# Attention units regrouped: four heads of two neighbouring rows in place of eight heads of one row

## The chip, the cores and the metric

The kernel runs on one core of a Trainium2 chip. The metric is the device time of one execution in microseconds. The core has a matrix engine (TensorE, PE in the profile; its weight loads are listed apart as PEld), a vector engine (VectorE, DVE), a scalar engine (ScalarE, ACT), GpSimd (POOL) and SyncE (SP), which issues most of the transfers. Each engine takes its instructions in program order; an instruction that is not ready holds up everything behind it on that engine.

## The reference

Three layers follow one another. The change touches only the first, attention over keys and values that are averaged in groups of eight:

```
B, H, S, D = q.shape                      # 8, 8, 576, 64
k_p = k.reshape(B, H, S // 8, 8, D).mean(axis=3)     # 72 pooled keys
v_p = v.reshape(B, H, S // 8, 8, D).mean(axis=3)
scores = (q @ k_p.transpose(0, 1, 3, 2)) / sqrt(D)
attn = softmax(scores)
x = (attn @ v_p).transpose(0, 2, 1, 3).reshape(B * S, H * D)   # 4608 x 512
x = moe(x)      # top 1 of 8 experts, 512 -> 1024 -> 512
out = swiglu(rmsnorm(x))                  # 512 -> 1536 -> 512
```

All data is float32. A float32 matmul appears in the trace as two instructions (two passes), so counts in the trace are twice those of the program.

## The kernel before

The attention stage takes about the first 225 us. It is cut into 36 units of 128 tokens: the eight batches form four pairs `m`, and each pair has nine units, four for each batch and a mixed one (`i == 8`) that holds the last 64 rows of both batches. A regular unit holds the rows 4p+r of its batch for one residue r and the 128 values of p, with all eight heads.

For each unit n the program emits `emit_qt` (turns q so that its 64 channels lie on partitions), `emit_sc` (scores of the eight heads against the 72 pooled keys, then maximum and subtraction on DVE), `emit_exp` (ACT), `emit_pt` (turns the probabilities), `emit_av` (product with the pooled values, normalising, and the gate's logits) and `store` (x to HBM). A loop over n interleaves five units:

```
emit_pt(n); emit_exp(n + 1); emit_qt(n + 3); run(n, "a"); emit_sc(n + 2); run(n, "b")
emit_av(n); store(n - 1); run(n, "c"); run(n, "d"); run(n, "e")
```

`run(n, w)` emits whatever a table has planned at place w of step n. The table `ORDER` gives each preparation step its place as a number i, step i // 5 and letter i % 5, one number for the first pair and one for the later ones: loads of k, v, q (`k0`, `v0`, `q00` ..., issued by SP), the pooling sums (`ksum`, `vsum`, on POOL and DVE), `kprep` (`prep_k`), `kend`, `vrows`, `vg` and `place`. The table `CW` does the same for the start of the expert layer: `choose`, `first_expert`, `first_tokens` (gathers token numbers, POOL), `first_rows`, then the loads and the splits of the first expert's weights into two parts (`split_w`, L147; half of them on POOL).

The turned keys of a batch lie in a tile `kbd` whose pair of heads is block diagonal: the even head of a pair on partitions 0 to 63 and its 72 columns, the odd one on partitions 64 to 127 and the next 72 columns, zeros elsewhere. One matmul with all 128 partitions then gives two heads' scores (L399), four matmuls a unit. For the mixed unit the two batches have their own keys, so each matmul is done for 64 tokens at a time (L402). q comes in tiles of four heads with four rows each next to one another in a partition (`load_q4`), so that 64 columns belong to one row and one head; a unit's q is turned by eight matmuls with 64 columns against the identity `ident` (L382). `prep_k` (L325) turns and sums the pooled keys with four matmuls per batch into PSUM tile `pk`, and two ACT copies place them in `kbd`. It is called once for each of the batches 2 to 7, and once more for the last rows of those six batches (`GB`). PSUM tiles `pq`, `pp` and `sc` have one buffer each.

The program ends its attention stage with units 32 to 35, while the first matmuls of the expert layer (L576, L545) already run in between.

Of the kernel before, what the change touches and what calls it, by code (L numbers as in the profile page):

```python
# [23 lines left out]
E = 8  # L24
# [57 lines left out]
def fused(ctx: ExitStack, tc: tile.TileContext, q, k, v, moe_w_gate, moe_w1, moe_w2,  # L82
# [106 lines left out]
    x_p = actx.enter_context(tc.tile_pool(name="xo", bufs=5))  # L189
# [3 lines left out]
    kbd = [at4.tile([128, 4, 2, NP], F32, name=f"kbd{i}") for i in range(3)]  # L193
# [18 lines left out]
    def load_q(b, rs=(0, 1, 2, 3)):  # L212
        t = kq["q", b] if ("q", b) in kq else [wtile(F32, f"q{z}") for z in range(2)]
        for r in rs:
            nc.sync.dma_start(
                out=t[r // 2][:, 512 * (r % 2):512 * (r % 2) + 512].rearrange("p (h d) -> p h d", h=H),
                in_=q[b, :, 0:512, :].rearrange("h (p r) d -> r p h d", r=4)[r])
        kq["q", b] = t

    def load_q2(b, j):  # L220

        t = kq["q", b] if ("q", b) in kq else [wtile(F32, f"q{z}") for z in range(2)]
        nc.sync.dma_start(
            out=t[j].rearrange("p (h n) -> p h n", h=H),
            in_=q[b, :, 0:512, :].rearrange("h (p r) d -> p h (r d)", r=4)[:, :, 128 * j:128 * j + 128])
        kq["q", b] = t
        two_rows.add((b, j))

    two_rows, four_rows = set(), set()

    def load_q4(b, j):

        t = kq.setdefault(("q", b), [])
        x = wtile(F32, f"q{j}")
        nc.sync.dma_start(
            out=x.rearrange("p (h n) -> p h n", h=4),
            in_=q[b, 4 * j:4 * j + 4, 0:512, :].rearrange("h (p r) d -> p h (r d)", r=4))
        t.append(x)
        four_rows.add(b)

    def load_mix(m):
        x = kv1.tile([128, DM], F32, tag="mxq", name="mxq")
# [52 lines left out]
    def turn(nm, b):  # L295
        s_ = kq[nm, "sum", b]
        pp = ps.tile([128, 4, NP], F32, tag="pp", name="pt" + nm)
        for hp in range(4):
            nc.tensor.transpose(pp[:, hp], s_[0:NP, 128 * hp:128 * hp + 128], ident[0:NP, 0:NP])
        return pp  # L300

    def rows_k(b):
        pp = turn("k", b)
        for z in range(2):
            nc.scalar.activation(out=kbd[b % 3][64 * z:64 * z + 64, :, z], in_=pp[64 * z:64 * z + 64],
                                 func=AF.Copy, scale=1.0 / 64)
# [13 lines left out]
    def prep_k(b):  # L320
        n = rows_of(b)
        s_ = kq["k", "sum", b]
        pp = ps.tile([128, 4, n // 2], F32, tag="pp", name="pk")
        for hp in range(4):
            nc.tensor.matmul(pp[:, hp], lhsT=s_[0:n, hp * 128:hp * 128 + 128], rhs=cc[0:n, C_PK:C_PK + n // 2])  # L325
        if isinstance(b, int):
            kb = kbd[b % 3]
            nc.scalar.copy(out=kb[0:64, :, 0, 0:64], in_=pp[0:64])
            nc.scalar.copy(out=kb[64:128, :, 1, 0:64], in_=pp[64:128])
        else:  # L330
            kt = kv1.tile([128, 4, n // 2], F32, tag="kt", name="kt")
# [4 lines left out]
    def end_k(b):  # L336
        kb = kbd[b % 3]
        kt, j = ends[b]
        for z in range(2):
            zs = slice(64 * z, 64 * z + 64)  # L340
            nc.scalar.copy(out=kb[zs, :, z, 64:NP], in_=kt[zs, :, 8 * j:8 * j + 8])
# [26 lines left out]
    def emit_qt(n):  # L368
        m, i = tl[n]
        pq = ps.tile([128, 4, 128], F32, tag="pq", name="pq")  # L370
        for hp in range(4):
            if i < 8:
                b = 2 * m + i // 4
                r = i % 4
                if b in four_rows or (b, r // 2) in two_rows:
                    for z in range(2):
                        h = 2 * hp + z
                        if b in four_rows:
                            src = kq["q", b][h // 4][:, 256 * (h % 4) + 64 * r:256 * (h % 4) + 64 * r + 64]
                        else:  # L380
                            src = kq["q", b][r // 2][:, 128 * h + 64 * (r % 2):128 * h + 64 * (r % 2) + 64]
                        nc.tensor.matmul(pq[64 * z:64 * z + 64, hp], lhsT=src, rhs=ident)  # L382
                    continue
                src = kq["q", b][r // 2][:, 512 * (r % 2) + 128 * hp:512 * (r % 2) + 128 * hp + 128]
# [3 lines left out]
        qt = at_p.tile([128, 4, 128], F32, tag="qt", name="qt")  # L388
        nc.scalar.copy(out=qt, in_=pq)
        qts[n] = qt  # L390

    def emit_sc(n):
# [3 lines left out]
        for hp in range(4):  # L396
            o = sc[:, hp // 2, 144 * (hp % 2):144 * (hp % 2) + 144]
            if i < 8:
                nc.tensor.matmul(o, lhsT=qt[:, hp], rhs=kbd[(2 * m + i // 4) % 3][:, hp])  # L399
            else:  # L400
                for z in range(2):
                    nc.tensor.matmul(o[64 * z:64 * z + 64], lhsT=qt[:, hp, 64 * z:64 * z + 64],  # L402
                                     rhs=kbd[(2 * m + z) % 3][:, hp])
# [983 lines left out]
```

## Time and profile before

| | us |
|---|---|
| median of 3 runs | 1653.56 (1651.57 to 1657.29) |
| the profiled execution | 1648.6 |
| its span | 1646.8 |
| PE busy | 1591.5 (97% of the span) |
| PEld busy | 1374.9 (83%) |
| DVE busy | 846.8 (51%) |
| ACT busy | 500.4 (30%) |
| POOL busy | 261.1 (16%) |

These are averages over three layers. The change lies in the first 225 us, where the chain that ended last, DVE, POOL and the transfers have quite other shares than over the whole span, so the stage has to be read by itself. The mean granted clock over the span is 0.99 of full speed.

### The profile page before, as it was taken

How to read it: one execution, taken by the hardware profiler on the slowest of the kernel's cores; microseconds unless marked ns; L12 is line 12 of the kernel's file. 1: busy time of each engine (PE TensorE's matmuls, PEld its weight loads, DVE VectorE, ACT ScalarE, POOL GpSimd, SP SyncE). 2: the span in 40 equal slices, each digit the busy share in tenths (PEclk: the TensorE clock that was granted, in tenths of full speed). 3: DMA queues.
4: the chain of work that ended last, by engine and by line, in shares of the span. 5: the costliest groups of instructions: out<-in, count | busy, mean ns of one | idle time of the engine just before them, and what ended most of it. 6: DMA issues, size and time to landing. Idle time of an engine off the chain costs nothing. (4 is left out here: it accounts for less than half of the span.)

```text
span 1646.8 us, 26476 instructions
## 1 busy us (share of the span) xinstructions
PE 1591.5 (97%) x9323; PEld 1374.9 (83%) x9323; DVE 846.8 (51%) x1796; ACT 500.4 (30%) x1052; POOL 261.1 (16%) x362
## 2 busy tenths in 40 slices
PE   9999989999999989998999999999999999999997
PEld 6888978978888888888888888888888888888886
DVE  7678876688757687224333433334343333443222
ACT  3545633455434453231212112121221212122121
POOL 5767551111111101103000000000000000000000
PEclk9999999999999999999999999999999999999999
DMA  7977866476746463319201100010010001000000
GB/s 207 266 185 174 181 93 212 133 269 219 259 127 234 144 230 119 71 34 322 58 13 27 26 14 26 13 39 13 20 33 13 26 13 38 14 1 26 0 26 14
DMA packets 125373, 161.97 MB, mean 98 GB/s; under 512 B 38544, under 2 KB 83728, under 8 KB 125216
## 3 DMA queue, kind: packets, MB, share of 16 engines
q1 hardware_dynamic: 113440, 124.13, 27.0%
q0 software_dynamic: 11776, 35.91, 6.9%
q8 instruction: 78, 1.28, 0.3%
q14 instruction: 79, 0.65, 0.1%
HBM read 116.92 MB, written 43.08 MB: 97 GB/s over the span
## 5 line engine op out<-in xcount | busy, mean ns | idle before, releaser
L1284 DVE SCALAR_TENSOR_TENSOR th<-th,g 128x512 f32<-128x512 f32 (+1 forms) x120 | 76.1, 634 | 473.2 <-ACT th L1283 458.8
L1281 PE MATMUL g<-xh,rl 128*128 128x512 f32 (+1 forms) x576 | 217.3, 377 | 0.0
L1280 PE MATMUL g<-xl,rh 128*128 128x512 f32 (+1 forms) x576 | 217.3, 377 | 0.0
L1279 PE MATMUL g<-xh,rh 128*128 128x512 f32 (+1 forms) x576 | 217.2, 377 | 0.0
L1283 ACT ACTIVATE th<-g 128x512 f32<-128x512 f32 (+1 forms) x120 | 66.8, 556 | 466.4 <-PE g L1281 456.8
L1310 POOL DMA_INDIRECT out_dram<-o,tk x36 | 34.7, 963 | 815.6 <-ACT o L1309 789.2
L1305 PE MATMUL po<-rl,a 128*128 128x512 f32 x360 | 140.3, 390 | 1.4 <-DMA rl<-scr 1.4
L1304 PE MATMUL po<-rh,a 128*128 128x512 f32 x360 | 140.2, 389 | 0.0
L1306 PE MATMUL po<-rh,a 128*128 128x512 f32 x360 | 140.1, 389 | 0.0
L1280 PEld LDWEIGHTS g<-xl,rh 128*128 128x128 f32 x576 | 108.3, 188 | 20.3
L1279 PEld LDWEIGHTS g<-xh,rh 128*128 128x128 f32 x576 | 108.3, 188 | 20.3
L1281 PEld LDWEIGHTS g<-xh,rl 128*128 128x128 f32 x576 | 108.3, 188 | 20.0
L146 ACT CAST a<-th 128x512 fp32r<-128x512 f32 (+1 forms) x120 | 69.4, 578 | 167.2 <-DVE th L1285 167.2
L545 PE MATMUL p<-xh,w1h 128*128 128x256 f32 x672 | 109.4, 285 | 10.9 <-DVE hl L548 8.7
L147 DVE TENSOR_TENSOR a<-th,a 128x512 fp32r<-128x512 f32 (+1 forms) x120 | 76.7, 639 | 77.3 <-ACT a L146 77.3
L1279 PE MATMUL g<-xh,uh 128*128 128x512 f32 (+1 forms) x288 | 108.7, 378 | 1.7 <-DVE th L1285 1.7
L1281 PE MATMUL g<-xh,ul 128*128 128x512 f32 (+1 forms) x288 | 108.6, 377 | 0.0
L1280 PE MATMUL g<-xl,uh 128*128 128x512 f32 (+1 forms) x288 | 108.6, 377 | 0.0
L545 PE MATMUL p<-xh,w1l 128*128 128x256 f32 x672 | 108.0, 284 | 0.0
L545 PE MATMUL p<-xl,w1h 128*128 128x256 f32 x672 | 107.3, 282 | 0.0
L545 PEld LDWEIGHTS p<-xh,w1h 128*128 128x128 f32 x672 | 93.3, 192 | 15.9 <-DVE hl L548 9.8
L548 DVE SCALAR_TENSOR_TENSOR hl<-p,hh 128x256 fp32r<-128x256 f32 x168 | 70.6, 421 | 64.1 <-ACT hh L547 58.4
(283 smaller groups left out, 3013.0 us busy)
## 6 DMA issues: line engine op xcount, KB each, us to landing
st<-in_moe_w_dram SPq DMA_DIRECT2D x64, 512.0 KB
y_d<-ys SPq DMA_DIRECT2D x39, 257.0 KB
v<-in_v_dram SPq DMA_DIRECT2D x32, 288.0 KB
y<-y_d SPq DMA_DIRECT2D x68, 128.0 KB
x_d<-x SPq DMA_DIRECT2D x32, 260.0 KB
q<-in_q_dram SPq DMA_DIRECT2D x15, 512.0 KB
scr<-uh SPq DMA_DIRECT2D x13, 512.0 KB
scr<-ul SPq DMA_DIRECT2D x13, 512.0 KB
```

Source lines behind the costliest of these rows:

```text
L146: nc.scalar.copy(out=hi, in_=src)
L147: eng.tensor_tensor(out=lo, in0=src, in1=hi, op=ALU.subtract)
L545: nc.tensor.matmul(a, lhsT=w[d][:, fs], rhs=x[:, d], start=j + d == 0, stop=j == 2 and d == 3)
L548: nc.vector.scalar_tensor_tensor(out=lo, in0=a, scalar=0.0, in1=hi, op0=ALU.max, op1=ALU.subtract)
L1279: nc.tensor.matmul(g[:, j], lhsT=wh[:, sl], rhs=hi[:, d], start=d == 0, stop=False)
L1280: nc.tensor.matmul(g[:, j], lhsT=wh[:, sl], rhs=lo[:, d], start=False, stop=False)
L1281: nc.tensor.matmul(g[:, j], lhsT=wl[:, sl], rhs=hi[:, d], start=False, stop=d == 3)
L1283: nc.scalar.activation(out=th, in_=g[:, 0], func=AF.Tanh, scale=0.5)
L1284: nc.vector.scalar_tensor_tensor(out=th, in0=th, scalar=1.0, in1=g[:, 0], op0=ALU.add, op1=ALU.mult)
L1304: nc.tensor.matmul(po, lhsT=a[:, 0, tsl], rhs=wh[:, sl], start=c == 0, stop=False)
L1305: nc.tensor.matmul(po, lhsT=a[:, 0, tsl], rhs=wl[:, sl], start=False, stop=False)
L1306: nc.tensor.matmul(po, lhsT=a[:, 1, tsl], rhs=wh[:, sl], start=False, stop=c == NC2 - 1)
```

## The change

A regular unit now holds four heads (g = i % 2) of two neighbouring rows (j = i % 4 // 2). The 128 columns of q that lie next to one another are two rows of one head, so that one transpose of 128 columns turns them; row 0 lands on partitions 0 to 63, row 1 on partitions 64 to 127. Four transposes turn a unit's q. Scores take the 64 partitions of one row for one head: eight matmuls with 128 weight columns and 72 columns of keys, alternating between the lower and the upper partitions (z), each z with its own PSUM bank. For that the keys of a head must lie on both halves of the partitions. `kbd` becomes `[128, 8, 72]`: column h holds head h on one half and its neighbour on the other, which needs seven full matmuls and two half ones in `prep_k` where there were four, followed by one ACT copy. `rows_k` (batches 0 and 1) turns its sums twice, with the second turn in `pq`. The mixed unit keeps its layout and goes to 16 matmuls with 72 columns each, against a zero padded q in a tile `qz`; each time two POOL memsets write its zeros. The result x of two units is stored together, so `xo` holds three double tiles in place of five, and the gate's logits are reduced once for two units. The initial zeros of `kbd` are no longer written. Two places of `ORDER` change for the first pair: q01 from 25 to 20 and q11 from 36 to 24.

```diff
-    ("q00", 6, 11), ("q10", 15, 18), ("q01", 25, 28), ("q11", 36, 36)]
+    ("q00", 6, 11), ("q10", 15, 18), ("q01", 20, 28), ("q11", 24, 36)]
-    x_p = actx.enter_context(tc.tile_pool(name="xo", bufs=5))
+    x_p = actx.enter_context(tc.tile_pool(name="xo", bufs=3))
-    kbd = [at4.tile([128, 4, 2, NP], F32, name=f"kbd{i}") for i in range(3)]
+    kbd = [at4.tile([128, H, NP], F32, name=f"kbd{i}") for i in range(3)]
...
+    def both_k(b):
+        return kbd[b % 3].rearrange("p (h o) s -> p o h s", o=2)
+
+    def of_k(b, h, z):
+        return kbd[b % 3][64 * z:64 * z + 64, (h - z) % 8]
...
     def prep_k(b):
-        pp = ps.tile([128, 4, n // 2], F32, tag="pp", name="pk")
-        for hp in range(4):
-            nc.tensor.matmul(pp[:, hp], lhsT=s_[0:n, hp * 128:hp * 128 + 128], rhs=cc[0:n, C_PK:C_PK + n // 2])
+        pp = ps.tile([128, 2, 4, n // 2], F32, tag="pp", name="pk")
+        w = cc[0:n, C_PK:C_PK + n // 2]
+        for c in range(8):
+            o = pp[:, c % 2, c // 2]
+            if c < 7:
+                nc.tensor.matmul(o, lhsT=s_[0:n, 64 * c:64 * c + 128], rhs=w)
+            else:
+                for z in range(2):
+                    h = (7 + z) % 8
+                    nc.tensor.matmul(o[64 * z:64 * z + 64], lhsT=s_[0:n, 64 * h:64 * h + 64], rhs=w)
         if isinstance(b, int):
-            kb = kbd[b % 3]
-            nc.scalar.copy(out=kb[0:64, :, 0, 0:64], in_=pp[0:64])
-            nc.scalar.copy(out=kb[64:128, :, 1, 0:64], in_=pp[64:128])
+            nc.scalar.copy(out=both_k(b)[:, :, :, 0:64], in_=pp)
...
     def emit_qt(n):
             if i < 8:
-                        nc.tensor.matmul(pq[64 * z:64 * z + 64, hp], lhsT=src, rhs=ident)
+                j, g = i % 4 // 2, i % 2
+                src = kq["q", 2 * m + i // 4][g][:, 256 * hp + 128 * j:256 * hp + 128 * j + 128]
             nc.tensor.transpose(pq[:, hp], src, ident)
+            qt = wtile(F32, "qz").rearrange("p (z h t) -> p z h t", z=2, h=4)
+            for z in range(2):
+                nc.gpsimd.memset(qt[64 * (1 - z):64 * (1 - z) + 64, z], 0.0)
+                nc.scalar.copy(out=qt[64 * z:64 * z + 64, z], in_=pq[64 * z:64 * z + 64])
...
     def emit_sc(n):
-        for hp in range(4):
-            o = sc[:, hp // 2, 144 * (hp % 2):144 * (hp % 2) + 144]
-                nc.tensor.matmul(o, lhsT=qt[:, hp], rhs=kbd[(2 * m + i // 4) % 3][:, hp])
+        if i < 8:
+            for h in range(4):
                 for z in range(2):
+                    nc.tensor.matmul(sc[:, z, NP * h:NP * h + NP], lhsT=qt[64 * z:64 * z + 64, h],
+                                     rhs=of_k(2 * m + i // 4, 4 * (i % 2) + h, z))
+        else:
+            for h in range(H):
+                for y in range(2):
+                    ys_ = slice(64 * y, 64 * y + 64)
+                    nc.tensor.matmul(sc[ys_, h // 4, NP * (h % 4):NP * (h % 4) + NP],
+                                     lhsT=qt[:, h % 2, h // 2, ys_], rhs=kbd[(2 * m + y) % 3][:, h - h % 2])
...
     def store(n):
+        if i < 8 and i % 2 == 0:
+            return
+            for z in range(2):
+                nc.sync.dma_start(out=rows[:, 2 * j + z], in_=xf[:, z])
```

What stands on PE in steps 4 and 5 of the loop, before (`pq` is the turned q, `sc` the scores, `pk` the turned keys, of sums `sk` for one batch and `se` for the last rows; a count is that of the program, half of that in the trace):

```order
L423 MATMUL pt<-cc,pe 72x128 x8
L382 MATMUL pq<-cc,q_200 64x128 x4
L382 MATMUL pq<-cc,q_202 64x128 x4
L347 MATMUL pvg<-wg,vt 72x16 x4
L399 MATMUL sc<-kbd_129,qt 128x144 x4
L433 MATMUL av<-vau_134,ptsb 128x73 x8
L325 MATMUL pk<-cc,sk 128x64 x4
L325 MATMUL pk<-cc,se 128x48 x4
```

And the same stretch of the changed program:

```order
L418 MATMUL pt<-cc,pe 72x128 x8
L372 MATMUL pq<-cc,q_203 128x128 x4
L342 MATMUL pvg<-wg,vt 72x16 x4
L391 MATMUL sc<-kbd_129,qt 128x72 x8
L428 MATMUL av<-vau_134,ptsb 128x73 x8
L321 MATMUL pk<-cc,sk 128x64 x7
L325 MATMUL pk<-cc,sk 64x64 x2
L321 MATMUL pk<-cc,se 128x48 x7
L325 MATMUL pk<-cc,se 64x48 x2
```

The order of the steps is the same; q is turned by four matmuls in place of eight, the scores take eight in place of four, and each call of `prep_k` nine in place of four.

On SP, which issues the loads in this order, the stretch around the moved load q11 stands before as follows (the 128x4x256 rows are loads of 512 KB, of k or of q; `q_732` is the load q01 and `q_927` is q11):

```order
L206 DMA k_728<-in_k_dram 128x4x256
L206 DMA k_730<-in_k_dram 128x4x256
L235 DMA q_732<-in_q_dram 128x4x256
L472 DMA x_d<-x 128x520
L206 DMA k_812<-in_k_dram 128x4x256
L206 DMA k_814<-in_k_dram 128x4x256
L472 DMA x_d<-x 128x520
L278 DMA v_850<-in_v_dram 72x2x512
...
L235 DMA q_927<-in_q_dram 128x4x256
```

And now, where `q_650` is q01 and `q_710` is q11:

```order
L217 DMA q_650<-in_q_dram 128x4x256
L482 DMA x_d<-x 128x520 x2
L217 DMA q_710<-in_q_dram 128x4x256
L206 DMA k_748<-in_k_dram 128x4x256
L206 DMA k_750<-in_k_dram 128x4x256
L206 DMA k_834<-in_k_dram 128x4x256
L206 DMA k_836<-in_k_dram 128x4x256
L482 DMA x_d<-x 128x520 x2
L258 DMA v_872<-in_v_dram 72x2x512
```

q11 is now issued ahead of four loads of k and four of v that it stood behind, and stores of x come in pairs.

On POOL, near the end of the attention stage, where the splits of the expert weights (`w1l`, `w2l`) and the writes of the token order (`ord_d`) stand, before:

```order
L147 TENSOR_TENSOR w1l_2732<-st_2494,w1h_2731 128x512 x2
L528 DMA ord_d<-tok,rpi 36864x1
L131 MEMSET spare 1x1
L147 TENSOR_TENSOR w2l_2804<-st_2562,w2h_2803 128x512 x2
L147 TENSOR_TENSOR w2l_2870<-st_2636,w2h_2869 128x512 x2
```

And now:

```order
L147 TENSOR_TENSOR w1l_2739<-st_2505,w1h_2738 128x512 x2
L380 MEMSET qz 64x512 x2
L538 DMA ord_d<-tok,rpi 36864x1
L131 MEMSET spare 1x1
L147 TENSOR_TENSOR w2l_2813<-st_2569,w2h_2812 128x512 x2
L147 TENSOR_TENSOR w2l_2887<-st_2643,w2h_2886 128x512 x2
```

The memsets of the last mixed unit's `qz` stand behind the splits of `w1l`; the scores of that unit, and all that follows them on PE, wait for these memsets.

## Rows read from the trace of the kernel before

**Rows 1.** Stretches of the attention stage, in windows; columns as in the header.

```profile
core 0: us, PE busy (x) PEld busy (x) DVE busy (x) ACT busy (x) POOL busy (x), PEclk, DMA share, GB/s
51.00:81.00 30.00, 29.28 (x296) 26.99 (x293) 19.58 (x41) 16.79 (x43) 24.58 (x32) 1.00 1.03 270
81.60:85.60 4.00, 0.24 (x8) 0.02 (x2) 2.82 (x6) 1.27 (x3) 3.77 (x5) 1.00 0.73 116
85.70:89.10 3.40, 3.40 (x21) 3.07 (x21) 0.22 (x1) 0.59 (x1) 3.24 (x5) 0.50 0.91 206
89.10:165.00 75.90, 73.03 (x727) 67.16 (x727) 61.25 (x147) 39.04 (x101) 49.86 (x70) 1.00 0.73 179
```

**Rows 2.** PE's timeline around its longest wait: start, length, instructions, [idle before <-releaser].

```profile
85.59 1.04 PE L382 MATMUL pq<-cc,q 128*64 128x128 f32 x8 [3.76 <-DMA q<-in_q_dram]
...
92.43 0.82 PE L423 MATMUL pt<-cc,pe 128*96 128x128 f32 x6
93.20 1.09 PE L382 MATMUL pq<-cc,q 128*64 128x128 f32 x16
94.22 1.25 PE L399 MATMUL sc<-kbd,qt 128*128 128x144 f32 x8
95.31 1.00 PE L325 MATMUL pk<-cc,sk 128*128 128x64 f32 x8
96.14 1.71 PE L441 MATMUL av<-both,ptsb 96*128 96x146 f32 x12
```

**Rows 3.** PE's timeline, 46 to 75 us.

```profile
46.33 1.90 PE L433 MATMUL av<-vau,ptsb 72*128 72x73 f32 x16
48.07 1.05 PE L325 MATMUL pk<-cc,sk 128*128 128x64 f32 x8
49.95 1.09 PE L325 MATMUL pk<-cc,se 96*128 96x48 f32 x8 [0.83 <-ACT kbd L329]
...
51.75 0.60 PE L387 MATMUL pq<-cc,mxq 128*128 128x128 f32 x4
52.19 1.15 PE L399 MATMUL sc<-kbd,qt 128*128 128x144 f32 x8
53.17 1.66 PE L359 MATMUL pv<-vau,both 72*96 72x146 f32 x12
54.67 1.90 PE L433 MATMUL av<-vau,ptsb 72*128 72x73 f32 x16
...
58.08 1.15 PE L402 MATMUL sc<-kbd,qt 128*64 128x144 f32 x16
59.16 1.11 PE L359 MATMUL pv<-vau,both 72*96 72x146 f32 x7
...
74.88 1.10 PE L325 MATMUL pk<-cc,sk 128*128 128x64 f32 x8
```

**Rows 4.** POOL's timeline, the ends of the sums of k of batches 2 and 3.

```profile
47.25 0.72 POOL L268 TENSOR_TENSOR sk<-k 128x256 f32<-128x256 f32 x1
...
70.75 0.72 POOL L268 TENSOR_TENSOR sk<-k 128x256 f32<-128x256 f32 x1
```

**Rows 5.** The issues of q01 and q11 in the timeline of SP's queue.

```profile
58.03 1.24 SPq L235 DMA_DIRECT2D q<-in_q_dram  x1
...
68.52 0.40 SPq L235 DMA_DIRECT2D q<-in_q_dram  x1
```

**Rows 6.** POOL's timeline: first gather of token numbers, last `w1l` splits.

```profile
165.31 1.00 POOL L637 DMA_INDIRECT tok<-ord_d,i  x1 [0.56 <-DVE mx L406]
...
206.03 2.52 POOL L147 TENSOR_TENSOR w1l<-st,w1h 128x512 fp32r<-128x512 f32 x2
```

**Rows 7.** PE's timeline in the last four units.

```profile
206.12 1.20 PE L402 MATMUL sc<-kbd,qt 128*64 128x144 f32 x16
208.00 1.73 PE L441 MATMUL av<-vbd,ptsb 96*128 96x146 f32 x12 [0.67 <-ACT xt L579]
...
211.74 0.71 PE L545 MATMUL p<-xt,w1h 128*128 128x256 f32 x4 [1.20 <-DVE rs L448]
```

More of the change, by code (lines that the diff above doesn't have):

```diff
@@ L210, in load_k, with load_q @@
             t.append(x)
[L212 to L222, printed above, removed]
-        nc.sync.dma_start(
[L224 to L239, printed above, removed]
+    def load_q(b, g, j=None):
+        t = kq["q", b] if ("q", b) in kq else kq.setdefault(("q", b), {})
+        if g not in t:
+            t[g] = wtile(F32, f"q{g}")
+        c = slice(0, 256) if j is None else slice(128 * j, 128 * j + 128)
+        nc.sync.dma_start(
+            out=t[g].rearrange("p (h n) -> p h n", h=4)[:, :, c],
+            in_=q[b, 4 * g:4 * g + 4, 0:512, :].rearrange("h (p r) d -> p h (r d)", r=4)[:, :, c])
     def load_mix(m):
-        x = kv1.tile([128, DM], F32, tag="mxq", name="mxq")
+        x = wtile(F32, "mxq")[:, 0:DM]
         for i in range(2):
@@ L293, in sum_rows, with turn @@
         eng.tensor_tensor(out=o, in0=x[:, :, 0], in1=x[:, :, 1], op=ALU.add)
-    def turn(nm, b):
+    def turn(nm, b, odd=False):
         s_ = kq[nm, "sum", b]
-        pp = ps.tile([128, 4, NP], F32, tag="pp", name="pt" + nm)
+        pp = ps.tile([128, 4, NP], F32, tag="pq" if odd else "pp", name="pt" + nm)
         for hp in range(4):
-            nc.tensor.transpose(pp[:, hp], s_[0:NP, 128 * hp:128 * hp + 128], ident[0:NP, 0:NP])
-        return pp
+            c = 128 * hp + 64 * odd
+            if c + 128 <= DM:
+                nc.tensor.transpose(pp[:, hp], s_[0:NP, c:c + 128], ident[0:NP, 0:NP])
+            else:
+                for z in range(2):
+                    h = (7 + z) % 8
+                    nc.tensor.matmul(pp[64 * z:64 * z + 64, hp], lhsT=s_[0:NP, 64 * h:64 * h + 64],
+                                     rhs=ident[0:NP, 0:NP])
+        return pp
+    def both_k(b):
+        return kbd[b % 3].rearrange("p (h o) s -> p o h s", o=2)
+    def of_k(b, h, z):
+        return kbd[b % 3][64 * z:64 * z + 64, (h - z) % 8]
     def rows_k(b):
[L303 to L306, printed above, removed]
+        for odd in range(2):
+            pp = turn("k", b, odd)
+            nc.scalar.activation(out=both_k(b)[:, odd], in_=pp, func=AF.Copy, scale=1.0 / 64)
     def rows_v(b):
@@ L336, in end_k @@
     def end_k(b):
-        kb = kbd[b % 3]
         kt, j = ends[b]
-        for z in range(2):
-            zs = slice(64 * z, 64 * z + 64)
-            nc.scalar.copy(out=kb[zs, :, z, 64:NP], in_=kt[zs, :, 8 * j:8 * j + 8])
+        nc.scalar.copy(out=both_k(b)[:, :, :, 64:NP], in_=kt[:, :, :, 8 * j:8 * j + 8])
     def prep_vg(b):
@@ L440, in emit_av @@
                 if i < 8:
-                    nc.tensor.matmul(o, lhsT=sb[:, g, c], rhs=vbd[(2 * m + i // 4) % 3][:, g, c], **kw)
+                    nc.tensor.matmul(o, lhsT=sb[:, g, c], rhs=vbd[(2 * m + i // 4) % 3][:, i % 2, c], **kw)
                 else:
@@ L459, in emit_av @@
             ac = a4[:, :, :, 0:D]
-        nc.vector.tensor_tensor(out=xf[:, 0:DM].rearrange("p (a h d) -> p a h d", a=2, h=4), in0=ac,
-                                in1=rs.to_broadcast([128, 2, 4, D]), op=ALU.mult)
-        done[n] = xf
+        xo = xf[:, 0, 0:DM].rearrange("p (a h d) -> p a h d", a=2, h=4) if i == 8 else \
+            xf[:, :, 256 * g:256 * g + 256].rearrange("p z (h d) -> p z h d", h=4)
+        nc.vector.tensor_tensor(out=xo, in0=ac, in1=rs.to_broadcast([128, 2, 4, D]), op=ALU.mult)
+        done[n] = xf, lh
     done = {}
     def store(n):
-        xf = done.pop(n)
-        nc.scalar.copy(out=xf[:, DM:XW], in_=lgs[:, n])
         m, i = tl[n]
+        if i < 8 and i % 2 == 0:
+            return
+        xf, lh = done.pop(n)
         if i < 8:
-            b = 2 * m + i // 4
-            nc.sync.dma_start(
-                out=x_d[b * S:b * S + 512, :].rearrange("(p r) d -> p r d", r=4)[:, i % 4], in_=xf)
+            b, j = 2 * m + i // 4, i % 4 // 2
+            nc.scalar.copy(out=xf[:, :, DM:XW], in_=lgs[:, n - 1:n + 1])
+            rows = x_d[b * S:b * S + 512, :].rearrange("(p r) d -> p r d", r=4)
+            for z in range(2):
+                nc.sync.dma_start(out=rows[:, 2 * j + z], in_=xf[:, z])
         else:
+            nc.scalar.copy(out=xf[:, 0, DM:XW], in_=lgs[:, n])
             for z in range(2):
                 t0 = (2 * m + z) * S + 512
-                nc.sync.dma_start(out=x_d[t0:t0 + 64, :], in_=xf[64 * z:64 * z + 64])
+                nc.sync.dma_start(out=x_d[t0:t0 + 64, :], in_=xf[64 * z:64 * z + 64, 0])
     def route_steps(n0, n1):
@@ L683, in fused @@
     for j in range(2):
-        steps[f"q{j}"] = lambda b, j=j: load_q4(b, j)
+        steps[f"q{j}"] = lambda b, j=j: load_q(b, j)
     for r in range(4):
@@ L773, in fused @@
     nc.gpsimd.tensor_copy(out=band[:, NP:2 * NP], in_=ident[0:NP, 0:NP])
-    for t in kbd[1:]:
-        nc.gpsimd.memset(t, 0.0)
     emit_qt(1)
```

61 lines of the change are left out of this document (30 added, 31 removed).

## The prediction

> **What bounds the kernel now.** The page's busy shares average three layers, and the chain of waits that ended last runs through the last layer, so neither says what the attention stage is worth. I read that stage by windows first [rows 1], then PE's timeline where a window shows PE idle, then POOL's and SP's timelines for whoever PE waited on. In the windows the reader is to see that PE is the bound of most of the stage: 29.28 of 30 us from 51 to 81 us, 73.03 of 75.9 from 89 to 165, while DVE has 61.25 in the latter and POOL 24.58 in the former, neither far off. One stretch differs: from 81.6 to 85.6 us PE has 0.24 us of work, and from 85.7 to 89.1 it is fully busy at a granted clock of 0.50, the lower of its two levels [rows 1]. The timeline names the wait: the second half of a unit's turn of q waits 3.76 us for a load of q [rows 2], which is q11, issued at 68.52 [rows 5]. So a saving on PE counts where PE is the bound, and is lost at each place where PE meets something that doesn't come earlier. Two such places are known: the first `prep_k` at 48.07, which starts 0.10 us after POOL ends its sum at 47.25 + 0.72 = 47.97 [rows 3, 4], and the end of the stage, where POOL works off the weight splits.
>
> **A regular unit.** From the start of the turned probabilities to the end of the scores it takes 95.31 - 92.43 = 2.88 us: 0.77 for six transposes, 1.02 for the turn of q, 1.09 for the scores [rows 2]. Rates of steady stretches, from start to start: a transpose of 128 columns 0.44 / 4 = 0.11; a pass with 128 weight columns and 73 moving ones (48.07 - 46.33) / 16 = 0.109; one with 146 moving columns (54.67 - 53.17) / 12 = 0.125 [rows 3]. By these the unit would take 6 x 0.11 + 8 x 0.109 + 8 x 0.125 = 2.53, where I take a pair of the turn's 64-column passes as one slot of 0.109; the other 0.35 I put down to the array changing to halves and back (an estimate). The changed unit needs 6 + 4 transposes, 1.10, and 16 score passes with 128 weight columns and 72 moving ones. If the two halves of the partitions work side by side, these are eight slots of 0.109, 0.87, and with the same 0.35 for the change of shape, the sum is 2.32: 0.56 less, say 0.55. If they go one after the other, they are 16 x 0.109 = 1.74, the sum is 3.19, and each unit is 0.31 longer. Rows of halves are not in the trace of before; the nearest rows are halves of the columns: 16 passes of 144 columns in 59.16 - 58.08 = 1.08 [rows 3], 0.0675 each against 0.125 for whole ones, so two at a time. But there a moving stream of 144 columns hides the weight loads; here 72 columns don't. I take side by side, and keep the other as a rival.
>
> The Trainium skill, page "TensorE: Matmul & The Clock Gate", section "LDWEIGHTS (loading the stationary operand)", has the time of a weight load set by its columns and not by its partitions, so a load for 64 partitions would save nothing; that speaks against the change. The passes with 72 partitions and 128 weight columns at 0.109 agree in that they are no shorter than whole transposes at 0.11 [rows 3]. The page "TensorEngine Tiling (Array Packing)", section "Key Properties", says that different tiles may load and multiply in parallel, by which the loads of the two halves overlap; by the first rule alone, with one load at a time, a unit would be 0.31 longer, by both 0.55 shorter.
>
> **`prep_k`.** Four matmuls, eight passes, took 96.14 - 95.31 = 0.83 [rows 2]. Now there are 14 whole passes, 14 x 0.104 (0.83 / 8) = 1.45, a pair of half ones twice, about 0.1, and one change of shape there and back, 0.3 at the same estimate: 1.9, or +1.05 each, for seven calls (two of them at 48 to 51 us, one at 74.88, the next at 95.31). One ACT copy of twice the columns replaces two, on half the partitions each; I count nothing, since ACT is busy 39.04 of 75.9 us [rows 1].
>
> **The mixed units.** 32 passes of 72 columns for 16 of 144 (1.08). By moved columns alone no change; by number of passes +1.08; I take +0.3. Their q is copied in two ACT copies, which are no more elements. The memsets of `qz` have no row; they lie between nothing and the 2.52 / 2 = 1.26 us of a split over 128x512 [rows 6], each for half the partitions; I take 0.5 each. Except at the end they are hidden, as POOL has 5 of 30 us free at its fullest.
>
> **The stages.** (a) 0 to 51 us: what PE gains early is lost at the wait for POOL's sum at 47.97, whose loads don't come earlier. After it stand two calls of `prep_k`, +2.1 at most; the 0.83 us wait between them for the copies out of the one buffer [rows 3] may shrink, with one copy in place of two. +1.5. (b) 51 to 81 us, PE the bound: five units, -2.75, one `prep_k`, +1.05, one mixed unit, +0.3: -1.4. (c) 81.6 to 85.6: q11 landed at about 85.59, 17.1 us after its issue at 68.52; now it stands one store behind q01, which was issued at 58.03 [rows 5]. Issued by about 60 and as slow, it lands at 77, four us before it is wanted. The wait of 3.76 goes, and with it the 3.40 us at half clock [rows 1], which at full clock are 1.70: -5.46, say -5.5. (d) 86 to 165: 12 units -6.6, three `prep_k` +3.15, one mixed +0.3, -3.15, of which DVE (61.25 of 75.9 busy, and it must keep up) lets through about 80%: -2.5. (e) The end: POOL's row from the first gather of tokens to its last `w1l` split takes 206.03 + 2.52 - 165.31 = 43.2 us [rows 6], and none of it becomes shorter. PE came to the scores of the last mixed unit 206.12 - 165.31 = 40.8 us after the same gather [rows 6, 7]; with six units and one `prep_k` less it comes some 2 us sooner, and now waits for the memsets behind those splits, until 44. The scores thus end about 3.4 us later against the gather than before. Behind them PE already waited 0.67 and 1.20 us [rows 7], of which much may be swallowed: +0.9 to +2.6, I take +1.8. The 1.20 is a wait on a chain through DVE that itself shifts, so I do not count it whole.
>
> Sum: 1.5 - 1.4 - 5.5 - 2.5 + 1.8 = -6.1. The profiled execution took 1648.6 (span 1646.8), 5 us under the median of the runs; against its own time the change gives 1642.5, against the median 1653.56 it gives **1647.5**. Later layers are not touched.
>
> **The rivals.** *Halves one after the other (slower).* The place is every unit's scores. With +0.31 for a unit in place of -0.55: (b) 5 x 0.31 + 1.35 = +2.9, (c) -5.5, (d) 3.7 + 3.45 = +7.2, (a) +2.5 as the units around the first `prep_k` aren't shorter, (e) PE is then no sooner, some 6 x 0.31 + 1.05 = +2.9. Sum +10.0: 1663.6. It decides from the point where 16 passes take longer than about 1.45 us (the 0.55 gained is then gone), and is whole at 1.74. For it speaks that only the loads, 128 columns wide, can set 0.109 where just 73 columns move [rows 3]; against it the column halves' 0.0675. Chance 0.22.
>
> *The wait moves (no change).* q11 goes ahead of four loads of 512 KB of k and of four of v, in a stretch where the transfer share is 1.03 at 270 GB/s [rows 1]. One such load takes 1.9 us there, so k of batches 3 and 4 come 2 to 4 us later. The sum of batch 3 ended at 70.75 + 0.72 = 71.47 and was wanted at 74.88 [rows 3, 4], a slack of 3.4. If k is later by more than that, or q11 itself takes over 21 us to land, PE waits again for 3 to 4 us and drops its clock: -6.1 + 5.5 = -0.6, 1653. The same time comes out if the change of shape costs twice my estimate. Chance 0.22.
>
> *More than forecast.* The change of shape costs nothing with row halves, and the memsets at the end don't delay anything: -0.35 for 17 units kept, -1.8: about 1641. Chance 0.05.
>
> **Chances and range.** The forecast itself gets 0.51; its own range is 1641 to 1651, from the ends of (a), (e) and of the mixed units (2.2 us together) and a third of the unit's estimate either way. The range for 8 in 10 reaches from 1640 to 1665, which takes in the slower rival. A measurement of this kernel tells some 0.3%, 5 us, from no change: below 1648.6, up to 1658.5, above. Faster: 0.6 of the forecast and all of the last case with a part of the second, 0.41. Slower: the serial rival and a little, 0.23. The rest, 0.36, is no telling change.
>
> **What would show it.** In the changed profile: a unit's eight score matmuls should take about 0.87 to 1.0 us from start to start, and the turn 0.44 (1.74 and up for the scores is the serial rival); no wait of PE for q near 82 us, and a granted clock of 1.00 in the stretch after; `prep_k` about 1.9 us; PE waiting 3 to 5 us at the scores of the last mixed unit, with POOL's memset as the releaser. The prediction is wrong if the loads of halves don't overlap, if a wait for k or q returns between 70 and 90 us, or if PE's gain in (d) turns into waits for DVE.

## The result

The changed kernel took 1663.0 us (median of 4 runs, 1659.1 to 1667.8), 1.0059 times the kernel before, with a 95% interval of 1.0031 to 1.0087. It is slower, where 1647.5 and faster was forecast. The time lies in the forecast's wide range, near the 1663.6 of the serial rival, but not by that rival's mechanism. Of the runs below, two executions far above all others (2258 us of the kernel before, 4086 us of `old_turn`) are left out.

The profiled execution took 1659.1 us (span 1657.3, 10.5 over before). The stretches that answer to [rows 1], and those around them, in windows of the changed kernel:

```profile
core 0: us, PE busy (x) PEld busy (x) DVE busy (x) ACT busy (x) POOL busy (x), PEclk, DMA share, GB/s
0.00:30.00 30.00, 26.52 (x159) 15.48 (x160) 16.64 (x17) 7.61 (x14) 13.45 (x26) 0.89 0.83 208
30.00:51.00 21.00, 20.68 (x204) 19.19 (x202) 17.07 (x32) 10.54 (x23) 12.50 (x16) 0.92 0.72 201
51.00:81.00 30.00, 27.47 (x239) 25.00 (x238) 14.60 (x34) 13.80 (x31) 18.25 (x23) 0.83 0.98 283
81.60:85.60 4.00, 4.00 (x48) 3.66 (x47) 3.52 (x8) 0.27 (x1) 3.59 (x7) 1.00 0.90 224
85.70:89.10 3.40, 3.40 (x37) 3.16 (x36) 1.76 (x2) 2.12 (x6) 3.17 (x5) 1.00 0.98 134
89.10:165.00 75.90, 72.34 (x742) 66.52 (x742) 61.45 (x148) 40.33 (x94) 57.05 (x80) 1.00 0.87 178
165.00:206.00 41.00, 35.99 (x369) 33.00 (x370) 28.41 (x81) 21.22 (x50) 22.25 (x30) 0.92 0.71 169
206.00:223.00 17.00, 14.14 (x123) 13.22 (x123) 11.48 (x32) 9.01 (x20) 14.64 (x17) 0.80 1.00 124
```

The column to read is PEclk. The wait for q and the half clock behind it are gone, as forecast. But the granted clock is below 1.00 in five other stretches; in the trace of before it had fallen only at that wait up to 223 us. From 51 to 81 us a mean of 0.83 is (1 - 0.83) x 2 x 30 = 10 us at the lower level, while PE has 27.47 us of work and 239 matmul passes, against 296 in the same stretch before.

The unit as a whole takes the time that was forecast, or a little less. PE's timeline of the changed kernel at full clock, a `prep_k` and then a unit:

```profile
83.25 1.77 PE L321 MATMUL pk<-cc,sk 128*128 128x64 f32 x14
84.95 0.34 PE L325 MATMUL pk<-cc,sk 128*64 128x64 f32 x4
85.22 0.86 PE L418 MATMUL pt<-cc,pe 128*96 128x128 f32 x6
...
89.34 0.82 PE L418 MATMUL pt<-cc,pe 128*96 128x128 f32 x6
90.00 0.60 PE L372 MATMUL pq<-cc,q 128*128 128x128 f32 x4
90.53 1.11 PE L391 MATMUL sc<-kbd,qt 64*128 64x72 f32 x16
91.58 0.69 PE L342 MATMUL pvg<-wg,vt 128*72 128x16 f32 x8
```

From the turned probabilities to the end of the scores it takes 91.58 - 89.34 = 2.24 us, against 2.88 [rows 2]: the turn 0.53, the scores 1.05. `prep_k` takes 85.22 - 83.25 = 1.97.

Two places are new. At the last mixed unit PE stands for POOL's memset (PE's timeline, then POOL's, of the changed kernel; they answer to [rows 6, 7]):

```profile
211.71 0.60 PE L586 MATMUL px<-cc,xg 128*128 128x128 f32 x4
214.94 0.35 PE L397 MATMUL sc<-kbd,qz 128*64 128x72 f32 x4 [2.63 <-POOL qz L380]
...
217.39 3.29 PE L436 MATMUL av<-vbd,ptsb 96*128 96x146 f32 x12
```

```profile
195.52 0.20 POOL L662 COPY lg<-xg 128x16 f32<-128x16 f32 x1 [10.33 <-DMA xg<-x_d,tok]
...
211.82 2.48 POOL L147 TENSOR_TENSOR w1l<-st,w1h 128x512 fp32r<-128x512 f32 x2
214.36 1.10 POOL L380 MEMSET qz<- 64x512 f32 x2
```

The memsets start right behind the splits, and PE right behind the first memset; what follows runs at half clock (3.29 us for what took 1.73 in [rows 7]). And near 182 us ACT and DVE stand still behind work of PE that ended before 181 us (timeline of all engines):

```profile
185.07 0.76 DVE L401 TENSOR_REDUCE mx<-sc 128x8 f32<-128x576 f32 x1 [3.78 <-remote]
...
186.50 0.41 ACT L305 ACTIVATE vt<-ptv 128x288 f32<-128x288 f32 x1 [6.12 <-remote]
```

That wait did not come back in the second trace of the same kernel. Stalls of this kind stand in other traces too: ACT stands still for 6.0 us before 183.4 us in `before_thin` and for 5.8 us before 190.8 us in `before_halves`, each with half clock around it.

### The profile page after: what moved, and what is told of

It is laid out like the page before. It is cut to its first block, busy times and chain, and to the rows that moved or that the text cites. A ratio compares the mean times of both kernels' runs of the same rounds, so it can differ in the third digit from the quotient of the medians.

```text
span 1657.3 us, 26538 instructions
## 1 busy us (share of the span) xinstructions
PE 1599.1 (96%) x9367; PEld 1379.5 (83%) x9367; DVE 838.4 (51%) x1779; ACT 498.8 (30%) x1028; POOL 264.9 (16%) x368
## 5 line engine op out<-in xcount | busy, mean ns | idle before, releaser
L555 PEld LDWEIGHTS p<-xh,w1h 128*128 128x128 f32 x672 | 93.9, 192 | 17.1 <-DVE hl L558 10.3
```

The lines of the kernel that those rows point to most:

```text
L555: nc.tensor.matmul(a, lhsT=w[d][:, fs], rhs=x[:, d], start=j + d == 0, stop=j == 2 and d == 3)
```

## The experiments

Each run lists the span and mean granted clock of each execution. Of these I work out the time at half clock, 2 x (1 - clock) x span, and the time less half of it, which is what an execution would take if the clock had stayed up and PE had been busy in all of that time. The clock is listed to 0.001, a step of 3.3 us at half clock. The factor of one half is an estimate: from execution to execution of one kernel, the time rises by 0.27 to 0.59 us for each us at half clock. So the last column is good to some us and no better. The rows below have the medians; ratios are to the kernel before as measured beside it, with their 95% intervals.

| kernel | runs | median us | ratio | half clock us | less half of it |
|---|---|---|---|---|---|
| before, beside the next four | 34 | 1646.9 | | 38 | 1628.3 |
| after_again | 12 | 1659.0 | 1.0071 (1.0044 to 1.0098) | 66 | 1627.1 |
| before_order | 12 | 1647.4 | 0.9993 (0.9969 to 1.0016) | 36 | 1629.1 |
| old_order | 12 | 1658.6 | 1.0076 (1.0046 to 1.0106) | 60 | 1628.9 |
| no_qz | 12 | 1660.5 | 1.0086 (1.0052 to 1.0121) | 66 | 1625.4 |
| before, beside the next four | 11 | 1647.0 | | 36 | 1629.8 |
| old_turn | 5 | 1669.5 | 1.0137 (1.0098 to 1.0175) | 53 | 1642.6 |
| old_turn_early | 6 | 1666.1 | 1.0100 (1.0072 to 1.0128) | 60 | 1636.1 |
| fill_waits | 6 | 1662.7 | 1.0104 (1.0064 to 1.0145) | 68 | 1630.5 |
| small_prep | 6 | 1665.5 | 1.0109 (1.0078 to 1.0141) | 80 | 1625.6 |
| before, beside the next three | 29 | 1648.3 | | 39 | 1629.7 |
| before_again | 12 | 1647.1 | 0.9996 (0.9979 to 1.0013) | 35 | 1630.4 |
| no_qz_fill | 12 | 1661.9 | 1.0081 (1.0056 to 1.0106) | 65 | 1628.1 |
| no_qz_steady | 12 | 1654.8 | 1.0049 (1.0027 to 1.0070) | 51 | 1628.8 |
| before, beside the next three | 21 | 1648.2 | | 36 | 1629.9 |
| no_qz_dense1 | 9 | 1657.9 | 1.0058 (1.0033 to 1.0082) | 53 | 1631.4 |
| no_qz_dense2 | 9 | 1659.2 | 1.0069 (1.0045 to 1.0092) | 46 | 1636.1 |
| before_dense2 | 10 | 1659.4 | 1.0074 (1.0051 to 1.0096) | 37 | 1640.7 |
| before, beside the next three | 19 | 1652.6 | | 43 | 1630.7 |
| before_thin | 12 | 1650.0 | 0.9985 (0.9968 to 1.0003) | 61 | 1620.1 |
| before_halves | 7 | 1660.9 | 1.0050 (1.0033 to 1.0067) | 56 | 1633.5 |
| before_thin_halves | 7 | 1669.8 | 1.0081 (1.0052 to 1.0109) | 97 | 1621.4 |

**A second trace of the changed kernel.** No edit.

> The changed kernel again, for a second trace. The first trace lost its time in four places: the start (+3.6 us at unit 0), the first calls of prep_k (+5 us between units 4 and 6), a wait of 4.6 us at 182 us in which ACT and DVE stood still behind work of PE that was long done, and the last mixed unit (+4.9 us); in four of these stretches the granted clock was 0.50. Theory 'clock': most of the loss is PE's clock falling at a new wait or a thin stretch, so the places come back with the waits. Theory 'accident': the start and the wait at 182 us belong to that execution alone. Clock: 1659 to 1668 us with the same places at half clock. Accident: the trace is 4 to 8 us shorter up to unit 28.

It was the slowest of its 12 executions, 1674.9 us, and shows the same loss larger. PE's timeline as the clock falls:

```profile
38.19 1.12 PE L391 MATMUL sc<-kbd,qt 64*128 64x72 f32 x16 [1.51 <-DVE rs L443]
39.35 2.73 PE L428 MATMUL av<-vau,ptsb 72*128 72x73 f32 x16
...
44.07 1.06 PE L372 MATMUL pq<-cc,q 128*128 128x128 f32 x4
...
45.92 1.99 PE L391 MATMUL sc<-kbd,qt 64*128 64x72 f32 x16
```

```profile
40.00:74.00 34.00, 33.31 (x197) 31.34 (x198) 11.54 (x26) 10.30 (x21) 16.61 (x21) 0.51 0.87 258
```

For 34 us PE is busy almost without a gap at the lower level (windows), and the scores take 1.99 us where they took 1.12; busy time alone doesn't show it. The late start (unit 0 at 20.5 us, 25.0 in the first trace, 21.3 before) and the wait at 182 us did not come back; the loss from unit 4 to 10 and the tail did. Over the 12 executions time and half clock go together (correlation 0.96, 0.55 us for each us at half clock).

**The order of the loads.** `before_order` puts `("q01", 20, 28), ("q11", 24, 36)` into the kernel before, `old_order` puts `("q01", 25, 28), ("q11", 36, 36)` back into the changed one.

> The kernel before, with q01 and q11 moved to the places 20 and 24 of the order table and nothing else. If the wait for q11 alone is what the move removes: about -5.2 us against before (3.76 of wait, 1.7 of half clock), 1647.5. Rival, the loads of k that stand behind q come too late: the wait moves to prep_k, and the time is within 2 us of before.

> The changed kernel with q01 and q11 back at places 25 and 36. If the order is worth the same here as I read it from the traces (the distance to before goes from +8.9 us at unit 10 to +3.7 at unit 11): about +5 us, 1668. If the changed kernel is so much later at this point that q11 is there anyway: no difference, 1663.

Neither moved the time. In `old_order` PE doesn't wait for q either (its timeline, the turns of the unit whose second half had waited and of the one behind it):

```profile
85.45 0.60 PE L372 MATMUL pq<-cc,q 128*128 128x128 f32 x4
...
91.64 0.66 PE L372 MATMUL pq<-cc,q 128*128 128x128 f32 x4
```

A unit now takes q of one group of four heads, so the second load is wanted a unit later, 6.2 us here. PE is also 4.4 us later at this place than in the trace of before (unit 10 at 84.8 against 80.4 us), as the expectation allowed for. The wait is thus gone without the new order; how much of that is the regrouping and how much PE's lateness is not separated. In `before_order` the wait is gone and unit 35 starts at 209.0 us, against 214.8 and 211.4 in the two traces of before, but PE's first matmul of the third layer starts at 745.0 against 745.3 and 744.4: a lead of 2.4 to 5.8 us that was not kept. Why is open.

**The memsets at the tail.** `no_qz`: the mixed unit's scores over 64 partitions and 64 tokens.

```diff
-            qt = wtile(F32, "qz").rearrange("p (z h t) -> p z h t", z=2, h=4)
...
+                        nc.tensor.matmul(sc[ys_, z, NP * hp:NP * hp + NP], lhsT=qt[64 * z:64 * z + 64, hp, ys_],
+                                         rhs=of_k(2 * m + y, 2 * hp + z, z))
...
+        po = pe if i < 8 else pe.rearrange("p a (b z) s -> p z (a b) s", z=2)
```

> The changed kernel without the zero padded qz and its memsets: the mixed unit's scores are taken over 64 partitions and 64 tokens at a time, each half of the partitions into its own bank, and the subtraction puts the heads back in order. Theory 'clock': the wait of 2.6 us at the last mixed unit goes, and with it the half clock in the 6.8 us behind it: -5 to -6 us, about 1657. Theory 'wait alone': -2.6 us, 1660. Nothing gained if PE then waits at the same place for the rows of x or for the weights: 1663.

Against the changed kernel measured beside it nothing is gained, and not because PE waits at the same place for something else: the wait is gone from the trace, and from unit 33 to 35 it wins 1.9 us on before where the changed kernel loses 4.1. But half clock stays at 66 us; in this trace 20 us of it came from 47 us on. So the memset is a real stall (2.9 to 15.5 us from start to start in the seven traces that have it, long where the rows `xg` land late and PE comes early), but not what sets the median.

**Waits, turn and prep_k.** `fill_waits` keeps PE at work in the early waits, `old_turn` and `old_turn_early` undo the turn of q, `small_prep` the matmuls of `prep_k`.

```diff
-        pp = ps.tile([128, 2, 4, n // 2], F32, tag="pp", name="pk")
+        pp = ps.tile([128, 2, 4, n // 2], F32, tag="pp" if isinstance(b, int) else "pq", name="pk")
+        if b == 2:
+            for r in range(8):
+                nc.tensor.transpose(pp[:, 0].rearrange("p c s -> p (c s)")[:, 0:128], ident, ident)
...
-    keep_warm(28)
+    keep_warm(34)
```

> The changed kernel with PE kept at work where the traces show it waiting early: 34 warm matmuls in place of 28 at the start, eight transposes of the identity ahead of the first prep_k, which waits for POOL, and the PSUM tile pq in place of pp for the second call, which waited 0.69 us for the copy out of pp. If the falls of the clock hang on these waits: no half clock from 45 us on and -5 to -9 us, 1652. If they hang on the thin units themselves: the first fall at about 30 us stays and with it most of the loss, 1657 to 1660.

```diff
-            nc.tensor.transpose(pq[:, hp], src, ident)
...
+                    nc.tensor.matmul(pq[64 * z:64 * z + 64, hp], lhsT=src[:, 64 * z:64 * z + 64], rhs=ident)
...
```

> The changed kernel with q of every regular unit turned in 16 passes of 64 columns, as before (the result is the same; all else is the changed kernel). Theory 'clock': the stretches at half clock between 30 and 100 us come because the thinner turn leaves too little running on PE; the full turn takes 0.5 us more in each of 32 units, up to 13 us of work, but the granted clock stays at 1.00 up to the tail, which gives back the 5 to 17 us that the falls of the two traces cost there: no slower than the changed kernel, 1650 to 1660, and clearly steadier from run to run. Theory 'work' (prep_k and the waits cost the time, the clock follows by accident): 12 us slower than the changed kernel, 1671.

> The same for the units up to 8 alone, where the clock fell. Clock: +4 us of work, -5 to -17 us of half clock: 1648 to 1656, and the granted clock is 1.00 from 20 to 100 us or nearly so. Work: +4 us, 1663.

```diff
+        for hp in range(4):
+            nc.tensor.matmul(pp[:, hp], lhsT=s_[0:n, hp * 128:hp * 128 + 128], rhs=cc[0:n, C_PK:C_PK + n // 2])
...
+        nc.scalar.copy(out=d[lo, 1], in_=pp[hi])
...
```

> The changed kernel with prep_k as before on PE (four matmuls, 0.83 us) and five ACT copies that place each head on both halves, in place of nine matmuls (1.97 us) and one copy. Theory 'work': seven calls by 1.1 us of PE, -6 to -8 us, 1652. Theory 'clock': the calls at 50 us are shorter, but PE has still less to do there; -2 us at most if the clock falls as before, 1657.

The fills gave no less half clock (68 us), and in their trace the clock still falls near 31 and 51 us, without a wait of PE before it; so these early waits are not what brings those falls. `old_turn` came out near the time that the theory of work gave (1669.5 for 1671), with less half clock (53) and 15 us more in the last column; `old_turn_early` was slower than either theory said, with a wait of 12 us for the memset in its trace. `small_prep`, forecast at 1652 or 1657, took 1665.5, with 14 us more at half clock than `after_again`. Turn and `prep_k` together suggest that half clock grows as PE has less to do; it was this reading that the rest of the runs tested.

**A second trace of before, and the parts put together.** `no_qz_fill` is `no_qz` with `fill_waits`, `no_qz_steady` that with the old turn in units 0 to 8.

> The kernel before, for a second trace: all distances so far are measured against one execution. If that one is typical, the wait for q11 at 82 us with 3.4 us of half clock behind it is there again, the attention stage ends within 2 us of the first trace, and the stretch from 340 to 733 us, in which every other trace lost 2 to 5 us against it, is as short again. If it isn't, the wait for q11 is missing or shorter: then moving q01 and q11 is worth less than the 5.5 us that I counted, which would explain why before_order was timed the same as before.

> no_qz and fill_waits together: without the memsets that PE waits for at the last mixed unit (2.9 to 15.5 us in the traces so far), and with PE at work in the early waits. By the traces' pieces against before: units 0 to 9 +2.5, the wait for q11 -5.5, units 11 to 27 -1.4, the rest 0 to -2: -5, 1642 to 1645. Theory 'clock and tail' wants that; theory 'work' (prep_k, and every gain of PE behind it lost to DVE and POOL) has it no faster than no_qz, 1660, as the fills only add work.

> The same, and the turn of q in 16 passes as before in the units up to 8, since the two kernels with the old turn had no half clock near 30 us, which the other traces of the changed kernel have. Work +4 us in units 0 to 8; if the fall near 30 us is what the thin turn brings, it costs 1.7 to 3.4 us and is gone: within 2 us of no_qz_fill. Granted clock 1.00 from 20 to 80 us.

In `before_again` the wait for q11 is there, shorter (2.95 us from start to start) and with no half clock behind it. `no_qz_fill` missed: its profiled execution was its fastest, 1648.5, but its median is 1661.9. `no_qz_steady` differs from it by the old turn alone, and is 7 us faster where 2 were allowed for, with 14 us less at half clock, and steadier (9 of 12 executions within 1651.7 to 1655.8). The two traces from 25 to 45 us, `no_qz_fill` first (windows):

```profile
25.00:45.00 20.00, 19.69 (x196) 18.20 (x195) 16.54 (x30) 10.54 (x23) 12.23 (x15) 0.91 0.71 207
25.00:45.00 20.00, 20.00 (x231) 18.16 (x231) 16.96 (x30) 9.59 (x20) 12.10 (x15) 1.00 0.72 220
```

PE hardly waits in either. The three traces with the old turn in these units keep a clock of 1.00 here; those of `after`, `old_order`, `no_qz`, `fill_waits` and `no_qz_fill` have 0.91, each with 0.5 us of idle PE at most. (`after_again` has 0.88, behind a wait of 1.5 us, and `small_prep`, with the short turn as well, 0.99.) In those five the fall comes with the short turn and without a wait. What it is worth in time is less sure: the same edit made the changed kernel no faster (`old_turn_early`, 1.0100, against 1.0071 of `after_again`).

**More work in each unit.** Matmuls of a tile of ones, overwritten by the turn; two in `no_qz_dense2` and `before_dense2`, one in `no_qz_dense1`.

```diff
+        for _ in range(2):
+            nc.tensor.matmul(pq, lhsT=ones, rhs=ones.unsqueeze(1).to_broadcast([128, 4, 128]))
```

> no_qz with two more matmuls ahead of each unit's turn of q (a tile of ones against itself, 512 bf16 columns each, about 0.43 us together; the result is overwritten and stays as it was). Over all runs so far the changed kernel has a median of 66 us at half clock against 36 of before, and what is left of the time without half of it is 1627 against 1629: the loss is the clock. Theory 'thin units' (the changed unit gives PE too little to do, and the clock falls again and again): half clock comes down to 35 to 45 us, and the time to 1652 or less in spite of 10 to 14 us of added work. Theory 'waits' (the clock falls at PE's waits only): half clock stays above 55 us and the time goes up, 1668.

> The same with one such matmul, about 0.21 us a unit. Thin units: between no_qz and no_qz_dense2 in half clock, about 50 us, time about 1655. Waits: 1664, half clock as in no_qz.

> The kernel before with the same two matmuls in each unit, as the price of the added work where the clock doesn't fall: half clock stays near 36 us, and the time goes up by the part of 14 us that isn't hidden behind DVE and POOL, 1655 to 1661, under either theory.

Half clock goes 66, 53, 46 us with none (`no_qz`), one and two, and stays at 37 in the kernel before, near what the theory of thin units had. The times missed its 1655 and 1652: they hardly move, since the work costs what the clock gives back (last column: 1625 to 1636 here, 1630 to 1641 in before).

**One part alone in the kernel before.** `before_thin` has only the short turn, `before_halves` only the scores over 64 partitions, `before_thin_halves` both; `prep_k`, the mixed units and the tail are those of before.

```diff
-                        nc.tensor.matmul(pq[64 * z:64 * z + 64, hp], lhsT=src, rhs=ident)
...
+                    nc.tensor.transpose(pq[:, hp], src, ident)
```

```diff
-                nc.tensor.matmul(o, lhsT=qt[:, hp], rhs=kbd[(2 * m + i // 4) % 3][:, hp])
...
+                    nc.tensor.matmul(sc[:, z, NP * hp:NP * hp + NP], lhsT=qt[zs, hp],
+                                     rhs=kbd[(2 * m + i // 4) % 3][zs, hp, z])
```

> The kernel before with the turn of q alone made as short as in the change: four transposes of 128 columns in place of 16 passes of 64 columns, from the same tiles (it turns other rows of q than the unit's own, so the values are not those of the reference; the amount of work on all other engines is the same). prep_k, the scores, the mixed units and the tail are those of before. Theory 'thin units': half clock rises from 36 to 50 us or more and the time from 1647 to 1650 or more, though PE has 0.5 us less to do in each of 30 units. Theory 'waits and prep_k': half clock stays at 36 and the time falls by 1 to 4 us, 1644.

> The kernel before with the scores alone taken over 64 partitions, eight matmuls of 72 columns in two banks in place of four of 144 (the same values; the subtraction puts the heads back in order). If the scores over half the partitions are what lowers the clock: half clock above 45 us and slower than before by 3 us or more. If it is the turn: half clock 36 us, time 1646 to 1648.

> Both together in the kernel before (values as in before_thin). Thin units: as the changed kernel, half clock 55 to 66 us and 1655 to 1660. Waits and prep_k: 36 us and 1643.

Each part alone brings half clock, 61 and 56 us against 43, and the two together 97, where 55 to 66 were expected. Windows of equal stretches, `before_again` first, then `before_thin`, `before_halves` and `no_qz_dense2`:

```profile
20.00:80.00 60.00, 57.57 (x576) 52.79 (x575) 42.61 (x86) 31.13 (x76) 41.91 (x54) 1.00 0.91 254
80.00:140.00 60.00, 56.45 (x563) 51.45 (x562) 47.03 (x105) 30.57 (x78) 41.26 (x56) 1.00 0.82 193
140.00:200.00 60.00, 57.62 (x576) 52.82 (x575) 48.82 (x138) 34.46 (x85) 38.07 (x50) 1.00 0.72 170
```

```profile
20.00:80.00 60.00, 54.85 (x462) 51.78 (x460) 42.08 (x87) 31.61 (x77) 40.97 (x53) 0.94 0.92 251
80.00:140.00 60.00, 51.85 (x395) 50.00 (x396) 40.71 (x96) 26.97 (x69) 40.50 (x55) 0.86 0.76 173
140.00:200.00 60.00, 51.81 (x417) 49.34 (x416) 43.84 (x120) 29.47 (x74) 30.93 (x44) 0.89 0.70 162
```

```profile
20.00:80.00 60.00, 57.73 (x545) 52.24 (x543) 35.89 (x72) 27.73 (x66) 34.33 (x42) 0.86 0.85 251
80.00:140.00 60.00, 56.34 (x615) 50.88 (x614) 42.33 (x96) 28.06 (x71) 43.18 (x61) 0.94 0.66 162
140.00:200.00 60.00, 55.98 (x558) 49.34 (x557) 43.70 (x117) 26.80 (x69) 32.16 (x45) 0.91 0.68 149
```

```profile
20.00:80.00 60.00, 58.45 (x561) 50.80 (x559) 38.37 (x73) 28.61 (x63) 35.16 (x44) 0.96 0.89 257
80.00:140.00 60.00, 59.23 (x613) 53.24 (x612) 46.62 (x103) 28.42 (x68) 47.26 (x64) 1.00 0.85 157
140.00:200.00 60.00, 56.57 (x574) 50.63 (x575) 48.27 (x123) 29.96 (x70) 31.42 (x44) 1.00 0.82 183
```

PE's busy share alone does not tell them apart: `before_halves` is about as busy as before and has half clock in all three stretches (half clock itself lengthens the busy time). In its timeline the clock falls right at the first `prep_k` of before, with the same wait as in [rows 3], where before keeps its clock:

```profile
47.12 1.05 PE L325 MATMUL pk<-cc,sk 128*128 128x64 f32 x8
49.01 1.94 PE L325 MATMUL pk<-cc,se 96*128 96x48 f32 x8 [0.83 <-ACT kbd L329]
...
53.44 1.99 PE L401 MATMUL sc<-kbd,qt 64*128 64x72 f32 x16
```

In `before_thin` it is waits that stand before the falls. PE idles 21.5 us between 20 and 200 us, 8.4 in `before_again`, and 10.8 of it are waits of the scores for DVE. Each of its five falls, near 39, 84, 118, 166 and 183 us, has a wait of PE of 1.3 to 3.9 us shortly before it (PE's timeline, two of them):

```profile
36.99 1.22 PE L398 MATMUL sc<-kbd,qt 128*128 128x144 f32 x8 [1.94 <-DVE rs L447]
...
117.90 2.19 PE L401 MATMUL sc<-kbd,qt 128*64 128x144 f32 x16 [3.88 <-DVE rs L447]
```

So the short turn brings half clock in two ways: without a wait, as in the two traces from 25 to 45 us above, and by letting PE run into waits, as here. How the half clock divides between them is not shown.

The short turn pays for its half clock (10.6 us less in the last column, a ratio about 1); the halves don't, as they save nothing worth the name (1.05 for 1.09 us).

## Why the prediction was wrong

**The unit: right in its sum, by sizes that cancel.** Forecast 2.32 us, measured 2.24. The scores took 1.05, not 0.87, and the turn 0.53, not 0.44, but I had added 0.35 for the change of shape, which is not there on top. The halves of the partitions work side by side: 16 passes of 128 weight columns in 1.05 are 0.066 each, against 0.109 for whole ones [rows 3]; a pair takes 0.131, a fifth more than one whole pass. That settles the serial rival, which wanted 1.74; its time, 1663.6, was met by accident. The Trainium skill, page "TensorEngine Tiling (Array Packing)", section "Key Properties", has different tiles load and multiply in parallel; with 0.066 us a pass the trace agrees.

**prep_k: right.** 1.97 for 1.9 us. The mixed units cost less than the +0.3: their 32 passes of scores took 1.22 us at full clock (66.89 us), where 16 had taken 1.15 [rows 3].

**The wait for q (c): right in the trace, wrong in its worth.** It goes, but it goes without the new order too, as `old_order` shows; and the 5.5 us that I took for it from one trace were 2.9 in the second (units 10 to 11, each against `before_order`), and left nothing in the time of `before_order`. This step carried nearly all of the forecast gain.

**The middle (d): right.** From unit 11 to 27 the first trace wins 1.9 us on before, the second 1.2; 2.5 was forecast. That the gain turns into waits for DVE, named as a sign of being wrong, shows in `before_thin` and not here.

**The tail (e): right in its place, too small.** From unit 33 to 35 the changed kernel loses 4.1 us in the first trace and 10 in the second, 1.8 was forecast. I took the 43.2 us of POOL's work [rows 6] as fixed, and PE as some 2 us sooner. POOL took 45.1 and 44.1 in the two traces (42 to 52 in the variants of the changed kernel), with waits of 10.3 and 11.2 us for the gathered rows, 8.7 before; PE stood ready 43.1 and 35.9 us behind the first gather, 40.8 before, and waited 2.6 and 8.8 us, with half clock behind. Taking the memsets away removed the stall, not the loss in the median time.

**The step that failed: the clock of the stages (a) and (b).** I counted PE's work at the full clock and let the clock change only for the better, in (c). For (a) and (b) together the sum has +0.1 us. Measured from unit 0 to unit 10, before the place of (c), the changed kernel loses 5.3 us on before in the first trace and 21.0 in the second. The granted clock there is 1.00 before, 0.89 and 0.72 now (windows): 14 and 45 us at half clock, worth 7 and 22, which is the loss.

Over all executions, the time less the clock's share is no different from before (1627.1 against 1628.3), while the time at half clock rises by 28 us in the median. At the 0.41 to 0.56 us for each that the five kernels of the first group show, this is 12 to 16 us, against the 12 between the medians. So the clock is what the time went to.

That the change itself brings the half clock is shown from both sides: more work per unit takes a part of it away (66, 53, 46 us), and the short turn or the halves, put alone into the kernel before, bring it (43 to 61 and 56, together 97). By what road is shown in part. The waits that `fill_waits` and `no_qz` take away are not needed for it, but waits as such are not ruled out: of the seven falls between unit 0 and 225 us in the two traces of the changed kernel, three come with waits of PE of at most 0.7 us shortly before them or with none, and four behind or in waits of 1.5 to 8.8 us. A wait does not decide it alone, as `before_again` kept its clock through 2.7 us of waiting for q. What is not shown is why the scores over half the partitions lower the clock although they give PE as much to do, and why in the same program half clock lasts 3.4 us in one execution and 34 in another. A changed kernel with the short turn and scores over all 128 partitions was not tried.

No version beat the kernel before.

## What to carry to other kernels

An engine that is 97% busy is no promise that less work makes it faster: look at the granted clock beside the busy time, in the stretch itself, before and after. A shorter instruction sequence can lose more to the clock than it saves, as here, and the loss shows as the same passes taking up to twice as long, not as idle time. An engine that gets faster may also meet waits that it did not meet before. Before a wait is counted as a gain, see in a second trace that it is there each time, and a few stages later whether its worth is still there.

## What the runs showed of the hardware

Matmuls over the two halves of the partitions, in two PSUM banks, overlap: 0.066 us a pass with 128 weight columns, against 0.109 for whole ones. They leave PE about as busy in the profile, and yet its clock was low for longer with them (56 us at half clock against 43 in the median, the work on all else the same). Once fallen, the clock stayed at 0.5 for 34 us of work almost without a gap (`after_again`, 40 to 74 us); in other traces it was up again after 3.4 us.
